# Second layer norm of a fused attention and MLP kernel: the turn of its rows moved from TensorE to VectorE, with the norm's scales passed through memory

## The chip, the cores and the metric

The kernel runs on one core of one Trainium2 chip. The metric is the device time of one execution in microseconds, median of several runs. Engines are named as the profile names them: PE is TensorE (PEld its weight loads), DVE is VectorE, ACT is ScalarE, POOL is GpSimd, SP is SyncE, which here only issues DMAs.

## The reference

One block of a transformer in f32, 2048 tokens of width 1024, 32 heads of 32, hidden width 3584:

```python
qkv = layernorm(x) @ wqkv
phi_q, phi_k = [softmax(t @ w_phi), softmax(-t @ w_phi)]  per head, t = q, k
o = (phi_q @ (phi_k^T v)) / (phi_q @ sum(phi_k) + 1e-6)
h = x + o @ wo
out = h + relu(layernorm(h) @ w1) @ w2
```

The layer norms have no weights: `(h - mean) / sqrt(var + 1e-5)` over the 1024 columns of a token. The change is in the second one, `layernorm(h)`.

## The kernel before, in words

**Matmuls.** Every product is made to f32 accuracy from two fp32r halves, a high part and a rest: `mm3` (L181) issues three matmuls of 512 columns, on L182, L183 and L184. Such a triple is called a step here. The work is a list of items, of 8 steps or (in the MLP) 4 steps each, in this order on PE: keys and values, queries, the output projection (`wo_item`, 32 items, the "wo stretch"), the up products of the MLP for token half b=0 and then b=1 (`up_item`, 98 items each), and the down products.

**What lies beside.** Everything else is hung on step numbers by a table: `when(step, f, ...)` (L904) calls f after that step of PE's list, and each engine gets its instructions in that order and runs them in order. `wo0` is the first step of the wo stretch, `up0` the first of the up products. What a step number fixes is therefore the order on each engine, and not a time: an instruction that waits holds up all behind it on its engine. SP issues nearly all DMAs in the same way, in one queue. The program gives each DMA one of eight semaphores in turn, so that a DMA waits for the landing of the one issued eight places before it.

**Attention inside the wo stretch.** For every pair of units u, POOL multiplies (`at_sums` L574, `at_den` L590, L594, `at_scale` L607, L612), DVE reduces (`at_reduce` L580), inverts (L597) and turns 32x32 blocks in place (`at_turn`, L618), then PE runs `at_num` (L632), ACT and DVE take its four banks (L639, L650). The chain goes POOL, DVE, POOL, DVE, POOL, DVE, PE. The last pair ends before the wo stretch does.

**Rows of h.** `wo_add` (L683, DVE) adds x to the projection in `xh`, `wo_store` writes it to memory (`hd`).

**Second layer norm before the change.** `ln_pair(b, i, stage)` (L691) does a pair of 128-token tiles, x1 and x2, four tiles of tokens apart; there are four pairs for each half b. Stage 0 reads both tiles back from `hd` (4 KB a token), stage 1 takes mean and variance (DVE, L221 and L223), stage 2 makes the two scales of a token (POOL, L230 to L232), stage 3 normalises (ACT, two instructions of 128x1024 on L238), stages 4 to 6 turn three half tiles and stage 7 the fourth: each is four 128x128 transposes on PE into one bank (L245, L713), copied back by ACT (L247, for b=0 L715 too). Stages 7 and 8 make sums and differences of quarters (DVE L717, L718, POOL L723, L724), since the MLP's products are made from seven combinations m of quarter matrices and not eight. `ln_store` writes the seven to memory (`hs`), `h_load` (L737) reads them into `hT[m]` in two parts g, `h_high` (ACT, L749) and `h_low` (DVE, L753) split them for the up products. The steps of the stages stand in the table `LN2` (L1050).

**Up products.** `up_item` keeps running sums in PSUM banks; ACT takes a bank (`up_take`, L776) after m = 1, 5, 6 and 4. After m=4 (the tile c21) the same bank is opened again one item later.

Of the kernel before, what the change touches and what calls it, by code (L numbers as in the profile page):

```python
# [140 lines left out]
def kernel(  # L141
# [60 lines left out]
    hs = {(b, m): dram.tile([P, 4, 512], F32, name=f"hs{b}_{m}") for b in range(2) for m in UP}  # L202
# [23 lines left out]
    def ln_power(key):  # L226

        mv = xst[key]
        sc = scx[:, key[1] - HT, :] if key[0] == "s" else lnp.tile([P, 2], F32, name="sc", bufs=4)
        pool.tensor_scalar_add(sc[:, 0:1], mv[:, 1:2], LN_EPS)  # L230
        pool.tensor_tensor(out=sc[:, 0:1], in0=sc[:, 0:1], in1=half, op=ALU.pow)
        pool.tensor_scalar(sc[:, 1:2], mv[:, 0:1], sc[:, 0:1], -1.0, op0=ALU.mult, op1=ALU.mult)  # L232
        xst[key] = sc

    def ln_norm(key):
        sc, src = xst.pop(("s", key[1]) if key[0] == "x" and key[1] >= HT else key), xin.pop(key)
        xnt[key] = src if key[0] == "h" else fp_ln.tile([P, D], F32, name="xn")
        act.activation(xnt[key], src, AF.Identity, bias=sc[:, 1:2], scale=sc[:, 0:1])  # L238

    def ln_turn(key, j, dst=None):  # L240
# [5 lines left out]
        if dst is None:  # L246
            act.activation(xn[:, j * 512:(j + 1) * 512], pt.rearrange("p k n -> p (k n)"), AF.Copy)  # L247
            return
# [441 lines left out]

    def ln_pair(b, i, stage):  # L691

        keys = [("h", HT * b + 4 * r + i) for r in range(2)]
        if stage == 0:
            for key in keys:
                ln_load(key, [hd[key[1]]])
        elif stage == 1:
            for key in keys:
                ln_stats(key)
        elif stage == 2:  # L700
            for key in keys:
                ln_power(key)
        elif stage == 3:
            for key in keys:
                ln_norm(key)
        elif stage in (4, 5, 6):
            ln_turn(keys[stage // 6], stage != 4)
        elif stage == 7:
            x1, x2 = (xnt[key] for key in keys)
            s12 = (mp or hp).tile([P, 2, 512], F32, name="s12", bufs=1)  # L710
            pt = tp_bank()
            for k in range(4):
                pe.transpose(pt[:, k * P:(k + 1) * P], x2[:, k * P:(k + 1) * P], ident)  # L713
            if b == 0:
                act.activation(s12[:, 1, :], pt, AF.Copy)  # L715
                pt = s12[:, 1, :]
            v.tensor_add(s12[:, 0, :], pt, x2[:, 512:])  # L717
            v.tensor_sub(x2[:, 0:512], x1[:, 0:512], pt)  # L718
            sums[b, i] = s12
        elif stage == 8:  # L720
            x1, s12 = xnt[keys[0]], sums[b, i]
            s4 = (mp or hp).tile([P, 512], F32, name="s4l", bufs=1)
            pool.tensor_tensor(out=s12[:, 1, :], in0=s12[:, 0, :], in1=x1[:, 0:512], op=ALU.subtract)  # L723
            pool.tensor_tensor(out=s4, in0=x1[:, 512:], in1=s12[:, 1, :], op=ALU.subtract)  # L724
            sums[b, i] = s12, s4

    def ln_store(b, i, j):

        x1, x2 = (xnt["h", HT * b + 4 * r + i] for r in range(2))
        s12, s4 = sums[b, i]  # L730
        m, t = ((1, x1[:, 0:512]), (5, s12[:, 0, :]), (6, s12[:, 1, :]), (2, x1[:, 512:]), (7, x2[:, 0:512]),
                (3, s4), (4, x2[:, 512:]))[j]
        sp.dma_start(hs[b, m][:, i, :], t)
# [3 lines left out]
    def h_load(b, m, g):  # L737

        lo = hT[m][:, 1, :, 2 * g * P:2 * (g + 1) * P].rearrange("p k (i n) -> p k i n", i=2)
        for i in range(2):  # L740
            sp.dma_start(f32(lo[:, :, i, :]), hs[b, m][:, 2 * g + i, :].rearrange("p (k n) -> p k n", k=4))
# [301 lines left out]
    for (t, hf), n in order:  # L1043
        do(max(n - 1, wo_first), -1, wo_load, t, hf)
        when(8 * n + (11 if n < wo_first + 2 else 9), wo_add, t, hf)
# [4 lines left out]
    LN2 = ((0, 9, 12, 17, 24, 25, 26, 27, 29, 36), (0, 18, 26, 32, 40, 42, 44, 46, 50, 60))  # L1050
    wo0 = 8 * wo_first
    up0 = 8 * first_up
    for i in range(4):
        for stage in range(9):
# [157 lines left out]
```

## Time and profile before

| what | value |
|---|---|
| median of 3 runs | 1896.47 us (1896.42 to 1900.21) |
| the profiled execution's own time | 1897.98 us |
| its span, first to last instruction | 1896.2 us |
| granted TensorE clock | 0.999 |
| busy: PE, DVE, POOL, ACT | 1880.8, 1050.0, 975.8, 740.3 us |
| wo stretch / b=0 up products begin | about 611 us / 818 us of the span |
| layer norm pairs, b=0 / b=1 | 664 to 803 us / 860 to 1054 us |

A row of the timeline gives start, duration, engine, line, operation, tiles and, in brackets, idle time before it and what ended that. A row of the grouped views ends in busy us, mean ns of one, and idle time before with its releasers. Consecutive matmuls overlap in the rows (0.39 us each, begun every 0.23 us), so that what a matmul takes of PE's time is the distance between starts.

### The profile page before, as it was taken

To read this page: it belongs to the slowest core of one execution; us is meant where nothing else is said; L and a number is where in the kernel's file an instruction comes from. 1 tells how busy PE (TensorE), PEld (TensorE's weight loads), DVE (VectorE), ACT (ScalarE), POOL (GpSimd) and SP (SyncE) were. 2 spreads that over 40 slices of the span, in tenths; PEclk is the share of its full clock that TensorE was granted. 3 is DMA by queue.
4 is the path that set the end of the run, shared out by engine and by line. 5 is a ranking of instruction groups with operands and counts; after the bars stand their busy time and mean duration, and the time that the engine had idled before them with its cause. 6 is when DMAs were issued, how large, how long until landed. Compare 5 with 4: busy or idle time off the path is not lost.

```text
span 1896.2 us, 31858 instructions
## 1 busy us (share of the span) xinstructions
PE 1880.8 (99%) x11640; PEld 1539.3 (81%) x11640; DVE 1050.0 (55%) x1685; ACT 740.3 (39%) x1258; POOL 975.8 (51%) x961
## 2 busy tenths in 40 slices
PE   8999999999999999999999999999999999999999
PEld 7777778877788788888888888888888888888887
DVE  6788678767679876555544563334433433343333
ACT  5322235222233112355445554444444444444442
POOL 4878742889946988423333222222244444444443
PEclk9999999999999999999999999999999999999999
DMA  6989785666665676796877996666677677777775
GB/s 222 285 280 310 232 284 197 194 192 209 199 207 177 199 240 221 248 272 219 272 233 238 301 285 202 181 194 202 217 240 217 198 234 236 239 212 219 216 216 178
DMA packets 292365, 432.17 MB, mean 228 GB/s; under 512 B 24048, under 2 KB 150000, under 8 KB 292208
## 3 DMA queue, kind: packets, MB, share of 16 engines
q1 hardware_dynamic: 275312, 413.36, 69.9%
q10 hardware_dynamic: 16896, 16.78, 2.5%
q8 instruction: 91, 1.49, 0.3%
q14 instruction: 66, 0.54, 0.1%
HBM read 292.68 MB, written 137.36 MB: 227 GB/s over the span
## 4 chain that ended last, share of the span: by engine, by line
PE 84%; POOL 6%; DMA 4%; issue 3%; DVE 2%; ACT 0%; SPq 0%; POOLq 0%; DVEq 0%; ACTq 0%
PE mm L182 21%; PE mm L183 21%; PE mm L184 21%; PE ac L184 4%; PE ac L182 4%; PE ac L183 4%; PE tp L182 2%; PE tp L184 2%; PE tp L183 2%; POOL w L129 2%; POOL b L361 2%; DMA b<-in_w_dram 1%; PE tp L245 1%; POOL ez L574 1%; DMA t<-b 1%
## 5 line engine op out<-in xcount | busy, mean ns | idle before, releaser
L129 POOL TENSOR_TENSOR w<-raw,w 128x512 fp32r<-128x512 f32 x355 | 475.2, 1340 | 722.0 <-ACT w L125 671.7
L125 ACT ACTIVATE w<-raw 128x512 fp32r<-128x512 f32 x686 | 409.1, 626 | 510.8 <-PE mm L184 245.4
L129 DVE TENSOR_TENSOR w<-raw,w 128x512 fp32r<-128x512 f32 x331 | 271.6, 821 | 529.4 <-ACT w L125 526.2
L182 PE MATMUL mm<-w,xT 128*128 128x512 f32 x768 | 308.5, 402 | 0.0
L183 PE MATMUL mm<-w,xT 128*128 128x512 f32 x768 | 301.5, 393 | 4.2 <-POOL w L129 3.8
L184 PE MATMUL mm<-w,xT 128*128 128x512 f32 x768 | 300.1, 391 | 0.0
L182 PE MATMUL mm<-hT,w 128*128 128x512 f32 x672 | 262.6, 391 | 0.0
L183 PE MATMUL mm<-hT,w 128*128 128x512 f32 x672 | 261.6, 389 | 0.3 <-DVE hT L753 0.3
L184 PE MATMUL mm<-hT,w 128*128 128x512 f32 x672 | 261.6, 389 | 0.0
L361 POOL TENSOR_TENSOR b<-b 128x256 f32<-128x256 f32 x224 | 181.1, 809 | 67.1 <-DMA b<-in_w_dram 57.6
L183 PEld LDWEIGHTS mm<-w,xT 128*128 128x128 f32 x768 | 144.7, 188 | 36.8 <-POOL w L129 7.3
L182 PEld LDWEIGHTS mm<-w,xT 128*128 128x128 f32 x768 | 144.6, 188 | 34.8 <-issue 4.2
L184 PEld LDWEIGHTS mm<-w,xT 128*128 128x128 f32 x768 | 144.6, 188 | 30.9
L182 PE MATMUL mm<-w 128*128 128x512 f32 x392 | 152.5, 389 | 0.0
L183 PE MATMUL mm<-w 128*128 128x512 f32 x392 | 152.5, 389 | 0.0
L184 PE MATMUL mm<-w 128*128 128x512 f32 x392 | 152.5, 389 | 0.0
L183 PEld LDWEIGHTS mm<-hT,w 128*128 128x128 f32 x672 | 126.2, 188 | 26.6 <-DVE hT L753 0.7
L184 PEld LDWEIGHTS mm<-hT,w 128*128 128x128 f32 x672 | 126.1, 188 | 26.3
L182 PEld LDWEIGHTS mm<-hT,w 128*128 128x128 f32 x672 | 126.2, 188 | 25.7
L452 POOL TENSOR_TENSOR zacc<-zacc,kphi 128x512 f32<-128x512 f32 x60 | 81.9, 1364 | 9.4 <-DVE kphi L444 9.4
L182 PEld LDWEIGHTS mm<-w 128*128 128x128 f32 x392 | 73.6, 188 | 15.3
L184 PEld LDWEIGHTS mm<-w 128*128 128x128 f32 x392 | 73.6, 188 | 15.3
(169 smaller groups left out, 3096.8 us busy)
## 6 DMA issues: line engine op xcount, KB each, us to landing
raw<-t SPq DMA_DIRECT2D x224, 256.0 KB, 4.0
raw<-ad SPq DMA_DIRECT2D x196, 256.0 KB, 3.0
raw<-in_w_dram SPq DMA_DIRECT2D x168, 256.0 KB, 3.1
b<-in_w_dram SPq DMA_DIRECT2D x56, 512.0 KB, 5.1
t<-b SPq DMA_DIRECT2D x56, 512.0 KB, 4.7
ad<-c SPq DMA_DIRECT2D x112, 256.0 KB, 3.6
ad<-s SPq DMA_DIRECT2D x84, 256.0 KB, 4.1
ed<-qe ACTq DMA_DIRECT2D x32, 512.0 KB, 4.6
```

Source lines behind the costliest of these rows:

```text
L125: nc.scalar.activation(w[:, 0, :], raw[1], AF.Copy)
L129: eng.tensor_tensor(out=w[:, 1, :], in0=raw[1], in1=w[:, 0, :].bitcast(F32), op=ALU.subtract)
L182: pe.matmul(ps, a_hi, b_hi, start=first, stop=False, skip_group_check=more)
L183: pe.matmul(ps, a_hi, b_lo, start=False, stop=False, skip_group_check=more)
L184: pe.matmul(ps, a_lo, b_hi, start=False, stop=last, skip_group_check=more)
L245: pe.transpose(pt[:, k, :], xn[:, (4 * j + k) * P:(4 * j + k + 1) * P], ident)
L361: pool.tensor_tensor(out=tsum[*u, *out], in0=tsum[*u, *a], in1=tsum[*u, *b], op=ALU.subtract)
L452: pool.tensor_tensor(out=zacc[s], in0=zacc[s], in1=phi_of[key], op=ALU.add)
L574: pool.tensor_tensor(out=ez, in0=e_q[u].rearrange("p (i h) s f -> p i (h s f)", i=4)[:, 2 * j:2 * j + 2, :], in1=zb[:, q, None, 256 * r:25 ...
```

## The change

The turn of the rows leaves PE. A tile is read back from `hd` in four DMAs of 32 partitions each, in pieces of 512 bytes, so that partition 32a+t gets the columns 128a to 128a+127 of each half of the row, for the four tokens 4t to 4t+3. DVE then turns the 32x32 blocks (`ln_swap`, one instruction of 128x1024 for each tile, written with a step of four elements), and the remaining exchange of chunks between partition groups is made by the addresses with which `h_load` reads `hs`: four DMAs of 32 partitions in place of two of 128. Since a partition now holds four tokens, mean and variance are taken earlier, on `xh` right after `wo_add` (`wo_stats`), the scales are made 4 steps later, written to memory four times over (`wo_scale`, 8 bytes a piece, into `scd`) and read back so that each partition has the scales of its four tokens (`scx`). ACT normalises in eight instructions of 128x256 for a pair. All sums stay, with other buffers as their places. The table `LN2` has new steps.

```diff
-    hs = {(b, m): dram.tile([P, 4, 512], F32, name=f"hs{b}_{m}") for b in range(2) for m in UP}
+    hs = {(b, m): dram.tile([P, 4, 4, P], F32, name=f"hs{b}_{m}") for b in range(2) for m in UP}
+    scd = {(b, i): dram.tile([2, 4 * P * 2], F32, name=f"scd{b}_{i}") for b in range(2) for i in range(4)}
...
+    def wo_stats(t, hf):
+        if hf == 0:
+            hst[t] = lnp.tile([P, 2, 6], F32, name="st", bufs=4)
+        v.bn_stats(out=hst[t][:, hf, :], in_=xh[t, hf])
+        if hf == 1:
+            xst["h", t] = mv = lnp.tile([P, 2], F32, name="mv", bufs=4)
+            v.bn_aggr(out=mv, in_=hst.pop(t))
+    def wo_scale(t):
+        dst = scd[t // HT, t % 4][t % HT // 4].rearrange("(a p s) -> p a s", a=4, s=2)
+        sp.dma_start(dst, xst.pop(("h", t))[:, None, :].to_broadcast([P, 4, 2]))
+    def ln_swap(dst, src):
+        v.transpose(dst.rearrange("p (c t g) -> p g c t", c=8, g=4), src.rearrange("p (g c k) -> p g c k", g=4, c=8))
     def ln_pair(b, i, stage):
...
+        if stage < 2:
+            t = tiles[stage]
+            xnt["h", t] = x = lnp.tile([P, D], F32, name="xin")
+            for a in range(4):
+                sp.dma_start(x[32 * a:32 * (a + 1)].rearrange("t (g r f) -> t g r f", g=4, r=2),
+                             hd[t].rearrange("(t g) (r a f) -> a t g r f", g=4, r=2, a=4)[a])
         elif stage == 2:
+            sp.dma_start(scx[:, 2 * i:2 * i + 2].rearrange("p r g s -> p r (g s)"),
+                         scd[b, i].rearrange("r (p f) -> p r f", f=8))
         elif stage == 3:
+            for r, t in enumerate(tiles):
+                for g in range(4):
+                    x, sc = xnt["h", t][:, 256 * g:256 * (g + 1)], scx[:, 2 * i + r, g]
+                    act.activation(x, x, AF.Identity, bias=sc[:, 1:2], scale=sc[:, 0:1])
+        elif stage == 4:
...
+            ln_swap(y2, x2)
+        elif stage == 5:
+            s, y1, y2 = sums[b, i]
+            ln_swap(y1, s)
+        elif stage == 6:
+            s, y1, y2 = sums[b, i]
+            v.tensor_add(s[:, 0:512], y2[:, 0:512], y2[:, 512:])
+            v.tensor_sub(y2[:, 0:512], y1[:, 0:512], y2[:, 0:512])
...
     def h_load(b, m, g):
-        for i in range(2):
-            sp.dma_start(f32(lo[:, :, i, :]), hs[b, m][:, 2 * g + i, :].rearrange("p (k n) -> p k n", k=4))
+        src = hs[b, m].rearrange("(a k) q i n -> q k a (i n)", a=4)
+        for q in range(4):
+            sp.dma_start(f32(hT[m][32 * q:32 * (q + 1), 1, :, 2 * g * P:2 * (g + 1) * P]),
+                         src[q, :, :, 2 * g * P:2 * (g + 1) * P])
...
+        when(added, wo_stats, t, hf)
+        if hf == 1:
+            when(added + 4, ln_power, ("h", t))
+            when(added + 12, wo_scale, t)
...
-    LN2 = ((0, 9, 12, 17, 24, 25, 26, 27, 29, 36), (0, 18, 26, 32, 40, 42, 44, 46, 50, 60))
+    LN2 = ((0, 3, 8, 16, 19, 21, 23, 25, 30), (0, 6, 10, 20, 26, 30, 34, 38, 46))
...
+        first, ln2 = wo0 + 64 + 40 * i, LN2[0] if i else (1, 4, 15, 21, 24, 26, 28, 30, 34)
```

On PE, where the turn of the first pair's tiles stood between the steps of a wo item, before (`tp<-ident,xin` are the transposes):

```order
L245 MATMUL tp<-ident,xin 128x128 x4
L182 MATMUL mm<-w,oT 128x512
L183 MATMUL mm<-w,oT 128x512
L184 MATMUL mm<-w,oT 128x512
L713 MATMUL tp<-ident,xin 128x128 x4
L182 MATMUL mm<-w,oT 128x512
```

In the changed kernel all 32 such rows are gone (7998 rows on PE in place of 8030), and nothing takes their place there.

On DVE, in the third pair of b=0, beside attention units 28 and 29 (`qe` their turn, `qtz` the reductions of the next two, `xh` the wo sums), before:

```order
L683 TENSOR_TENSOR xh<-mm,xh 128x512
L618 STREAM_TRANSPOSE qe<-qe 128x1024 x2
L683 TENSOR_TENSOR xh<-mm,xh 128x512
L580 TENSOR_REDUCE qtz<-ez 128x16 x2
L717 TENSOR_TENSOR s_8904<-s_8904,xin 128x512
L718 TENSOR_TENSOR xin<-xin,s_8904 128x512
L580 TENSOR_REDUCE qtz<-ez 128x16 x2
```

and in the changed kernel (`s_8880<-xin` and `xin<-xin` on L704 are the two swaps):

```order
L681 TENSOR_TENSOR xh<-mm,xh 128x512
L692 BN_STATS st<-xh 128x6
L704 STREAM_TRANSPOSE s_8880<-xin 128x4x256
L616 STREAM_TRANSPOSE qe<-qe 128x1024
L704 STREAM_TRANSPOSE xin<-xin 128x4x256
L616 STREAM_TRANSPOSE qe<-qe 128x1024
L733 TENSOR_TENSOR xin<-s_8880 128x512
L734 TENSOR_TENSOR s_8880<-xin,s_8880 128x512
L681 TENSOR_TENSOR xh<-mm,xh 128x512
L692 BN_STATS st<-xh 128x6
L695 BN_AGGR mv<-st 128x2
L578 TENSOR_REDUCE qtz<-ez 128x16 x4
```

Both swaps now stand ahead of an attention turn, and behind ACT's normalising.

On SP, just after the up products of b=0 have begun, where `hT7` and `hT3` are read for the first time (`raw` are weights), before:

```order
L741 DMA hT_9564<-hs_7_104 128x4x128 [waits DMAHW5_49,PE_49]
L741 DMA hT_9564<-hs_7_104 128x4x128 [waits DMAHW6_49]
L337 DMA raw<-t_2_312 128x512 [waits DMAHW7_49,Pool_49]
L741 DMA hT_9564<-hs_7_104 128x4x128 [waits DMAHW0_49]
L741 DMA hT_9564<-hs_7_104 128x4x128 [waits DMAHW1_49]
L337 DMA raw<-t_3_313 128x512 [waits DMAHW2_49,DVE_49]
L741 DMA hT_9565<-hs_3_105 128x4x128 [waits DMAHW3_49]
```

and in the changed kernel:

```order
L755 DMA hT_9630<-hs_7_104 32x4x256 [waits DMAHW0_49,PE_49]
L755 DMA hT_9630<-hs_7_104 32x4x256 [waits DMAHW1_49]
L755 DMA hT_9630<-hs_7_104 32x4x256 [waits DMAHW2_49]
L755 DMA hT_9630<-hs_7_104 32x4x256 [waits DMAHW3_49]
L335 DMA raw<-t_2_320 128x512 [waits DMAHW4_49,Pool_49]
L755 DMA hT_9630<-hs_7_104 32x4x256 [waits DMAHW5_49]
L755 DMA hT_9630<-hs_7_104 32x4x256 [waits DMAHW6_49]
L755 DMA hT_9630<-hs_7_104 32x4x256 [waits DMAHW7_49]
L755 DMA hT_9630<-hs_7_104 32x4x256 [waits DMAHW0_49]
L701 DMA scd_3_121<-sc 128x4x2 [waits DMAHW1_49]
L335 DMA raw<-t_3_321 128x512 [waits DMAHW2_49,DVE_49]
```

Each part g is four issues of 128 KB, in pieces of 1 KB, where it was two of 256 KB in pieces of 512 bytes; a scale write stands between them, and the turn of the eight DMA semaphores (DMAHW0 to 7) comes round after fewer bytes.

71 lines of the change are left out of this document (23 added, 48 removed).

## The prediction, as it was put on record before the run

> **What bounds the kernel now.** I read the page first: busy shares and slices.
>
> ```profile
> PE 1880.8 (99%) x11640; PEld 1539.3 (81%) x11640; DVE 1050.0 (55%) x1685; ACT 740.3 (39%) x1258; POOL 975.8 (51%) x961
> ...
> PE   8999999999999999999999999999999999999999
> ```
>
> PE is busy in 99% of the span and never under nine tenths after the first slice. Then who PE waits for, in the list of PE's waits:
>
> ```profile
> PE mm L183 <- POOL w L129: 3.8, 7, 1.4
> PE tp L245 <- ACT xn L238: 3.3, 2, 2.2
> ```
>
> These are the two largest entries of eight, 7.1 us. So PE's own instructions set the time, a microsecond off PE's list is a microsecond off the span, and the question is which waits grow. The same transposes grouped by form:
>
> ```profile
> L245 PE MATMUL tp<-ident,xin 128*128 128x128 f32 x96 | 14.4, 272 | 0.5 <-DVE oT L650 0.5
> L713 PE MATMUL tp<-ident,xin 128*128 128x128 f32 x32 | 4.8, 272 | 0.0
> ```
>
> Those 128 transposes, in 32 groups of four, are all that the change takes from PE.
>
> **What goes.** A row's duration is not its price, since matmuls overlap; the distance between starts is. PE's timeline at the first group:
>
> ```profile
> 681.32 0.39 PE L182 MATMUL mm<-w,oT 128*128 128x512 f32 x1
> 681.55 0.39 PE L183 MATMUL mm<-w,oT 128*128 128x512 f32 x1
> 681.78 0.40 PE L184 MATMUL mm<-w,oT 128*128 128x512 f32 x1
> 682.01 0.60 PE L245 MATMUL tp<-ident,xin 128*128 128x128 f32 x4
> 682.37 0.47 PE L182 MATMUL mm<-w,oT 128*128 128x512 f32 x1
> 682.68 0.39 PE L183 MATMUL mm<-w,oT 128*128 128x512 f32 x1
> ```
>
> From the L184 to the second matmul behind the group is 682.68 - 681.78 = 0.90 us; without a group two matmuls take 681.78 - 681.32 = 0.46 us. A group costs 0.44 us, four times 0.11 and not 0.27. 32 groups make 14.2 us, and the wait of 0.5 us for `oT` in the grouped row goes with them: **14.7 us** is the most that this edit can give.
>
> **What comes, engine by engine.** DVE gets two swaps a pair. The nearest row is the attention turn, the same operation on the same size, without the step of four elements in its output; beside it the sums that go on as they are and the statistics:
>
> ```profile
> L618 DVE STREAM_TRANSPOSE qe<-qe 128x1024 f32<-128x1024 f32 x28 | 34.3, 1232 | 15.8 <-POOL qe L612 14.6 <-POOL qe L602 1.2
> L221 DVE BATCH_NORM_STATS2 st<-xin 128x6 f32<-128x512 f32 x64 | 40.7, 676 | 7.9 <-DMA xin<-hd 7.0 <-DMA xin<-in_x_dram 0.8
> L223 DVE BATCH_NORM_AGGREGATE mv<-st 128x2 f32<-128x12 f32 x32 | 6.7, 209 | 1.4
> L718 DVE TENSOR_TENSOR xin<-xin,s 128x512 f32<-128x512 f32 x4 | 4.9, 1221 | 0.0
> ```
>
> No row shows the strided output. Below, a swap cannot take less than the 1.23 us of the dense one; above, the slower of the sums beside it has a mean of 1.22 us for 512 elements, 2.4 us for 1024. I take 1.23 us, the row of the same operation: 16 swaps, 19.7 us of DVE, up to 39. The Trainium skill, page "SBUF — State Buffer", section "Door 1: The DMA port swizzle (why `[64,N]` ≈ `[32,N]`)", says that SBUF is read in lines of 16 bytes and that every access to a new line pays; four f32 are one line, so by it each element of a swap pays. It gives no time, and no row here shows such a write. By it the sum below would end at the first rival's 1889.6 us, and without it at 1885.8.
>
> The statistics are as many as before, half of them (those of b=1) moved into the wo stretch: 16 on L692 and 8 small ones. ACT loses 24 copies of 0.6 us, with four more on L715, and has for the two normalising instructions of a pair (1.24 us each) eight of a quarter of the size:
>
> ```profile
> L247 ACT ACTIVATE xin<-tp 128x512 f32<-128x512 f32 x24 | 14.4, 599 | 19.5 <-PE tp L245 19.5
> L238 ACT ACTIVATE xin<-xin,sc 128x1024 f32<-128x1024 f32 x16 | 19.5, 1239 | 16.8 <-POOL sc L232 16.7
> L639 ACT ACTIVATE oT<-tp 128x256 fp32r<-128x256 f32 x32 | 10.6, 382 | 118.5 <-PE tp L632 113.0 <-PE ac L632 5.5
> ```
>
> A 128x256 one is between 0.31 us (a quarter) and 0.38 us; I take 0.38: 3.1 us a pair for 2.5. POOL's instructions are the same, the scales earlier. SP gets 128 more issues: 48 for the read-back, 16 scale writes, 8 scale reads, 56 for `hT`.
>
> **Three places where these can reach PE.**
>
> *Attention beside the pairs of b=0 (676 to 770 us).* Busy time by engine there:
>
> ```profile
> core 0: us, PE busy (x) PEld busy (x) DVE busy (x) ACT busy (x) POOL busy (x), PEclk, DMA share, GB/s
> 676.00:770.00 94.00, 93.51 (x1154) 75.80 (x1153) 65.06 (x113) 22.16 (x43) 81.66 (x105) 1.00 0.69 226
> 860.00:1050.00 190.00, 190.00 (x870) 157.37 (x869) 89.64 (x131) 94.34 (x155) 70.69 (x66) 1.00 0.74 237
> ```
>
> and, of the first of these stretches alone, the wo sums and the statistics:
>
> ```profile
> L683 DVE TENSOR_TENSOR xh<-mm,xh x14: 624/641/653, 680.0 to 768.9; 128x512 f32<-128x512 f32 x14
> L221 DVE BATCH_NORM_STATS2 st<-xin x8: 674/678/695, 705.8 to 742.9; 128x6 f32<-128x512 f32 x8
> ```
>
> Three pairs lie in the first stretch, so PE's list shrinks by 12 x 0.44 + 0.5 = 5.8 us to 88 us. POOL's 81.7 us stay: 93%. DVE gets six swaps (7.4 us) and, one for each wo sum, 14 statistics with 7 small ones for 8 with 4 (6 x 0.68 + 3 x 0.21 = 4.7 us): 65.1 + 12.1 = 77 us, 88%. Both still fit, but their chain has little slack; these are the turns of units 21 and 31 and the `at_num` that takes them:
>
> ```profile
> 698.11 1.25 DVE L618 STREAM_TRANSPOSE qe<-qe 128x1024 f32<-128x1024 f32 x1 [0.95 <-POOL qe L612]
> ...
> 767.76 1.25 DVE L618 STREAM_TRANSPOSE qe<-qe 128x1024 f32<-128x1024 f32 x1 [0.96 <-POOL qe L612]
> ```
>
> ```profile
> 700.93 0.34 PE L632 MATMUL tp<-qe,kvL 32*32 32x128 f32 x8
> ...
> 769.97 0.34 PE L632 MATMUL tp<-qe,kvL 32*32 32x128 f32 x8
> ```
>
> 700.93 - 699.36 = 1.6 us and 769.97 - 769.01 = 1.0 us. PE arrives 5.8 us earlier at the second. Part is made good: POOL stood idle here because DVE took statistics of rows still under way, and that place in DVE's list goes:
>
> ```profile
> 674.81 1.29 POOL L574 TENSOR_TENSOR ez<-qe,zb 128x512 f32<-128x512 f32 x1 [4.44 <-DVE qtz L580]
> ...
> 744.49 1.29 POOL L574 TENSOR_TENSOR ez<-qe,zb 128x512 f32<-128x512 f32 x1 [3.36 <-DVE qtz L580]
> ```
>
> Those two gaps are 7.8 us, more than the 4.8 us that lack (5.8 less the slack of 1.0); but a swap stands behind ACT, which stands behind two reads from memory, and all of DVE stands behind the swap, the next turn first. I leave **2 us** of the 5.8 lost here; the ends are 0 and all 5.8.
>
> *The first read of hT7.* It can only begin with the up products, and PE already waits for it by a hair:
>
> ```profile
> 839.72 0.39 PE L182 MATMUL mm<-hT,w 128*128 128x512 f32 x1
> 840.37 0.50 PE L183 MATMUL mm<-hT,w 128*128 128x512 f32 x1 [0.26 <-DVE hT L753]
> ```
>
> 840.37 - 839.72 is 0.65 us for 0.23. What is later by the change shows here at once; the bytes are the same, the issues double:
>
> ```profile
> hT<-hs SPq DMA_DIRECT2D x56, 256.0 KB, 6.1
> raw<-wpk SPq DMA_DIRECT2D x56, 128.0 KB, 3.3
> ```
>
> If a read of half the size lands like the other of 128 KB, in 3.3 us, eight places in flight carry as much as before. I put **1 us**, between 0 and 3.
>
> *ACT in b=1.* After m=4 ACT must empty the bank before PE opens it again:
>
> ```profile
> 1093.43 0.58 ACT L776 ACTIVATE c<-mm 128x512 f32<-128x512 f32 x1
> ```
>
> ```profile
> 1095.35 0.39 PE L182 MATMUL mm<-hT,w 128*128 128x512 f32 x1
> ```
>
> 1095.35 - 1094.01 = 1.3 us of slack. The third pair's eight normalising instructions are issued 4 steps (2.7 us) ahead of such a take and last 3.1 us, if rows and scales have landed; scales are asked for 10 steps (6.8 us) ahead. The second reads of hT, about 1063 to 1112 us, stand on ACT in the same way. **1 us** for both, between 0 and 4. In the rest of b=1 DVE has 190 - 90 = 100 us to spare, and the swaps cost nothing.
>
> **Sum.** 14.7 - 2 - 1 - 1 = 10.7 us. The profiled execution took 1897.98 us and would take 1887.3; it lies 1.5 us above the median, so that the median goes from 1896.47 to about **1885.8 us**. With the ends: 14.7 less 0 gives 1881.8, 14.7 less 12.8 gives 1894.6.
>
> **Rivals.**
>
> *The swaps go at half rate and DVE binds attention.* Where each element of a swap is a line of its own, 2.5 us a swap is twice the attention turn. DVE's 77 us become 85 of 88, and its waits for POOL (0.95 us before each second turn) find no room: the 5.8 us of that stretch come back whole. 14.7 - 5.8 - 1 - 1 = 6.9: **1889.6 us**. The rule on lines in the Trainium skill's page "SBUF — State Buffer" would have it so. For it speaks that nothing in the trace writes so; against it that DVE also gives up waits for rows from memory.
>
> *The eight places bind, and it is slower.* SP's rows for the first reads of hT7, hT3 and hT4 (16 DMAs, 12 of them `hT`) and for the second reads of all (59, 28 of them `hT`), first and last of each:
>
> ```profile
> 827.22 0.93 SPq L741 DMA_DIRECT2D hT<-hs  x2
> ...
> 838.47 1.04 SPq L741 DMA_DIRECT2D hT<-hs  x2
> ...
> 1063.79 2.47 SPq L741 DMA_DIRECT2D hT<-hs  x4
> ...
> 1111.91 1.10 SPq L741 DMA_DIRECT2D hT<-hs  x2
> ```
>
> They take 12 and 49 us now and will be 29 (12 more `hT`, a scale) and 87. If a landing took 6.1 us whatever the size, eight places would give 1.31 issues a us: 22 and 66 us, 10 and 17 us late. Weights are read far ahead; what `hT` has in hand I put at 3 us each time, so that PE loses 7 + 14 = 21 us. Against 14.7 less 2 that is 8 us slower, **1905 us**. It is no change at a landing of 5.5 us and slower from 5.8 on. The row of 3.3 us for 128 KB speaks against it; for it, that those went into 128 partitions and not 32.
>
> *The turn is not gone from PE's time.* Then the distance between matmuls there would stay and the time be 1896; the order has no row in the groups' place and PE has nothing else that waits, so I give it no more than 1 in 100.
>
> **Chances.** The forecast 0.63, with 1881.5 to 1889; DVE bound 0.18, up to 1893; still less than the forecast loses 0.04; the eight places, whole 0.07, in part 0.07; the turn not gone 0.01. About 0.2% (3.8 us) is what can be told from no change: faster 0.85, same 0.08, slower 0.07. The range leaves out the 0.15 above 1893 and a little below: 1881 to 1893.
>
> **What would show it.** PE's instructions fall to 11512, and where L245 and L713 stood starts are 0.23 us apart. The swaps' mean on L704 decides between 1.23 and 2.5 us. PE's waits at L632 name DVE or POOL if attention binds: 2 us in all by the forecast, 6 or more by the first rival. The landing of `hT<-hs` decides the second rival: 3.3 us or 5 and more, with PE's wait at the first matmul of m=7. At the openings of m=1 PE should wait under 1 us for ACT. I am wrong if PE waits 6 us at any one place, or if the swaps are past 2.4 us and L632 still waits for nothing.

## The result, and the profile after

The changed kernel takes **1946.28 us** (median of 4 runs, 1942.39 to 1949.42) against 1896.49 us (4 runs): a ratio of 1.0261, 95% interval 1.0249 to 1.0274. It is 50 us slower; 1885.8 had been forecast, with 1893 as the upper end. The profiled execution took 1949.42 us, its span is 1947.6 us and its mean granted clock 0.984 (0.999 before).

First the page of the changed kernel: PE's busy row, its slices and the granted clock in tenths.

```profile
PE 1891.1 (97%) x11512; PEld 1539.6 (79%) x11512; DVE 1085.4 (56%) x1701; ACT 736.2 (38%) x1278; POOL 974.2 (50%) x961
...
PE   8999999999999989979999999999999999999999
...
PEclk9999999999999989989999999999999999999999
```

The 128 transposes are gone (11512 instructions for 11640), yet PE's busy time has gone up by 10.3 us, since some of it went at a lower clock (below); and PE has two slices under nine tenths, at 682 and at 828 us, where before it had none after the first. Next, whom PE waits for (total, times, longest):

```profile
PE tp L630 <- issue: 10.5, 4, 6.9
PE mm L182 <- ACT c L791: 9.9, 4, 4.1
PE mm L182 <- ACT hT L764: 7.3, 2, 7.1
PE mm L182 <- DVE xh L681: 5.1, 2, 4.6
PE tp L630 <- DVE qe L616: 4.6, 4, 2.1
PE mm L183 <- POOL w L129: 3.4, 5, 1.4
PE mm L183 <- DMA hT<-hs: 2.7, 1, 2.7
```

Before, no entry was above 3.8 us. L630 is `at_num`, L764 and L768 the split of `hT`, L791 the taking of a bank. Where these waits lie, and what the DMAs move meanwhile, is shown by two stretches, the attention beside the pairs of b=0 and the first up products. Here they are in the changed kernel:

```profile
676.00:770.00 94.00, 81.96 (x959) 64.14 (x957) 63.15 (x102) 18.56 (x46) 69.06 (x83) 0.92 0.82 199
...
818.00:893.00 75.00, 59.17 (x232) 46.44 (x231) 34.16 (x40) 28.80 (x42) 21.38 (x22) 0.86 0.99 218
```

The second one before (the first stands in the prediction, with PE busy for 93.51 of 94 us):

```profile
818.00:893.00 75.00, 74.74 (x337) 61.57 (x336) 39.01 (x51) 41.26 (x65) 22.78 (x20) 1.00 0.81 246
```

PE loses 12 and 16 us there, at a clock of 0.92 and 0.86, and POOL and DVE do *less* in the first than before (69.1 for 81.7 us, 63.2 for 65.1). So DVE isn't overloaded: something makes all of them wait. The last two columns point to it: the DMA engines are busy for 82% and 99% of the time at 199 and 218 GB/s, where before 69% gave 226 and 81% gave 246. The same bytes take more of the engines' time.

**The attention wait, followed back.** PE's longest wait in the first stretch, from the timelines of PE, DVE, POOL, ACT and SP:

```profile
706.46 0.47 PE L630 MATMUL tp<-qe,kvL 32*32 32x128 f32 x8 [6.90 <-issue]
...
708.61 0.47 PE L630 MATMUL tp<-qe,kvL 32*32 32x128 f32 x8 [1.40 <-DVE qe L616]
```

```profile
692.13 2.00 DVE L704 STREAM_TRANSPOSE s<-xin 128x1024 f32<-128x1024 f32 x1 [10.64 <-ACT xin L722]
...
707.31 1.25 DVE L616 STREAM_TRANSPOSE qe<-qe 128x1024 f32<-128x1024 f32 x1 [0.95 <-POOL qe L610]
```

```profile
696.04 1.29 POOL L572 TENSOR_TENSOR ez<-qe,zb 128x512 f32<-128x512 f32 x1 [5.94 <-DVE qtz L578]
```

```profile
688.03 4.07 ACT L722 ACTIVATE xin<-xin,scx 128x256 f32<-128x256 f32 x8 [11.59 <-DMA xh<-in_x_dram]
```

```profile
663.70 7.24 SPq L713 DMA_DIRECT2D xin<-hd  x8
671.05 0.53 SPq L701 DMA_DIRECT2D scd<-sc  x1
...
672.95 0.37 SPq L701 DMA_DIRECT2D scd<-sc  x1
...
679.68 0.37 SPq L716 DMA_DIRECT2D scx<-scd  x1
```

Read from below: the scales are asked for at 679.68 us and ACT can only normalise at 688.03, some 8 us later. DVE has stood at the first swap since 681.5, the attention reductions (L578) behind it; POOL waits for those for 5.9 us, the turn of unit 21 ends at 708.56 and PE has waited since 699.6. The profile names "issue" and a read of `xh` as releasers. ACT doesn't use `xh`; of what it needs, the read of the scales came last, for it stands eight places behind the last read of the rows in SP's queue, so that those had landed when it was issued. A second read was late too: POOL had stood for 6.1 us, up to 686.34, for the attention's own read of `ed`. How much of PE's wait is due to which of the two this trace does not separate (a run below shows that late scales are enough).

**The first read of hT7.** The next large wait is at its first use:

```profile
876.40 0.80 PE L182 MATMUL mm<-hT,w 128*128 128x512 f32 x1 [7.11 <-ACT hT L764]
879.92 0.80 PE L183 MATMUL mm<-hT,w 128*128 128x512 f32 x1 [2.72 <-DMA hT<-hs]
```

```profile
863.35 5.31 SPq L755 DMA_DIRECT2D hT<-hs  x4
...
870.48 7.72 SPq L755 DMA_DIRECT2D hT<-hs  x8
```

Four and eight issues take 5.3 and 7.7 us, about a us each: SP waits at each for the landing of the one eight places before. The table of DMAs gives the landings (KB each, median us):

```profile
hT<-hs SPq DMA_DIRECT2D x112, 128.0 KB, 6.1
xin<-hd SPq DMA_DIRECT2D x64, 128.0 KB, 5.9
raw<-wpk SPq DMA_DIRECT2D x56, 128.0 KB, 3.7
scd<-sc SPq DMA_DIRECT2D x16, 4.0 KB, 8.4
scx<-scd SPq DMA_DIRECT2D x8, 8.0 KB, 6.5
```

A read of `hT` of half the size lands in the same 6.1 us as before, and a scale write of 4 KB, the smallest transfer of the program, takes the longest of these. Last, the two new groups on DVE and ACT:

```profile
L704 DVE STREAM_TRANSPOSE s<-xin 128x1024 f32<-128x1024 f32 x8 | 16.2, 2022 | 32.2 <-ACT xin L722 26.8 <-DMA hd<-xh 5.4
L722 ACT ACTIVATE xin<-xin,scx 128x256 f32<-128x256 f32 x64 | 32.5, 592 | 55.0 <-DMA scx<-scd 14.8 <-DMA xh<-in_x_dram 11.6 <-POOL ez L572 11.0
```

A swap takes 2.0 us, a normalising instruction 0.59.

**The clock.** After these waits PE goes slower for a while. The 13.7 us from 871.7 on, as a row of busy times, granted clock third from the end:

```profile
871.70:885.40 13.70, 6.28 (x14) 4.61 (x15) 5.76 (x7) 6.15 (x9) 1.80 (x1) 0.50 1.01 192
```

There matmuls begin 0.43 us apart instead of 0.23. Behind 600 us there are eight such stretches at 0.5, of 3.4 to 13.7 us, 61 us in all, each following one or more waits; before there was none. The account: the span grew by 51 us, and some 14 of saved transposes have to be added. PE's waits behind 600 us grew from 1.3 to 42.6 us, which makes 41 of these 65 us. For the other 24 there is the half clock: PE was busy for 44 of the 61 us, and half of that, an estimate of 22 us, is lost.

### The profile page after: what moved, and what is told of

Its sections match the earlier page's. It is cut to its first block, busy times and chain, and to the rows that moved or that the text cites. A ratio compares the mean times of both kernels' runs of the same rounds, so it can differ in the third digit from the quotient of the medians.

```text
span 1947.6 us, 31843 instructions
## 1 busy us (share of the span) xinstructions
PE 1891.1 (97%) x11512; PEld 1539.6 (79%) x11512; DVE 1085.4 (56%) x1701; ACT 736.2 (38%) x1278; POOL 974.2 (50%) x961
## 4 chain that ended last, share of the span: by engine, by line
PE 78%; DMA 9%; POOL 6%; issue 3%; DVE 2%; ACT 1%; SPq 1%; POOLq 0%; ACTq 0%; DVEq 0%
PE mm L182 19%; PE mm L183 19%; PE mm L184 19%; PE ac L184 3%; PE ac L183 3%; PE ac L182 3%; DMA hT<-hs 3%; PE tp L184 2%; PE tp L182 2%; PE tp L183 2%; DMA hd<-xh 2%; POOL b L359 1%; POOL w L129 1%; DMA xh<-in_x_dram 1%; POOL ez L572 1%
## 5 line engine op out<-in xcount | busy, mean ns | idle before, releaser
L129 DVE TENSOR_TENSOR w<-raw,w 128x512 fp32r<-128x512 f32 x331 | 276.4, 836 | 527.9 <-ACT w L125 527.5
L182 PE MATMUL mm<-hT,w 128*128 128x512 f32 x672 | 267.1, 398 | 22.4 <-ACT c L791 9.9
L183 PE MATMUL mm<-hT,w 128*128 128x512 f32 x672 | 265.8, 396 | 3.5 <-DMA hT<-hs 2.7
L184 PE MATMUL mm<-hT,w 128*128 128x512 f32 x672 | 265.1, 395 | 0.0
L182 PEld LDWEIGHTS mm<-hT,w 128*128 128x128 f32 x672 | 128.7, 192 | 53.0 <-ACT c L791 12.2
L183 PEld LDWEIGHTS mm<-hT,w 128*128 128x128 f32 x672 | 128.7, 192 | 31.6 <-DVE hT L768 4.3
L184 PEld LDWEIGHTS mm<-hT,w 128*128 128x128 f32 x672 | 128.6, 191 | 26.9
```

The lines of the kernel that those rows point to most:

```text
L129: eng.tensor_tensor(out=w[:, 1, :], in0=raw[1], in1=w[:, 0, :].bitcast(F32), op=ALU.subtract)
L182: pe.matmul(ps, a_hi, b_hi, start=first, stop=False, skip_group_check=more)
L183: pe.matmul(ps, a_hi, b_lo, start=False, stop=False, skip_group_check=more)
L184: pe.matmul(ps, a_lo, b_hi, start=False, stop=last, skip_group_check=more)
```

## The experiments

Theory 1: the scale writes, in pieces of 8 bytes, slow all other transfers. Theory 2: reads into 32 partitions land no faster for being smaller, and the eight semaphores bind (the second rival of the prediction). Theory 3: the swaps bind DVE (its first rival). Theory 4: each wait of PE costs a stretch at half clock besides.

### Each suspect taken out of the changed kernel

Without the scale writes (`scd` filled once from rows of x instead):

```diff
     def wo_scale(t):
-        dst = scd[t // HT, t % 4][t % HT // 4].rearrange("(a p s) -> p a s", a=4, s=2)
-        sp.dma_start(dst, xst.pop(("h", t))[:, None, :].to_broadcast([P, 4, 2]))
+        xst.pop(("h", t))
```

> The changed kernel without its 16 scale writes of 512 pieces of 8 bytes: the scales that ACT reads come from rows of x that are copied to scd once, early, so the true scales are left out; all reads, normalising and swaps stay. Theory 1 (the 8-byte writes slow every other transfer for several us each, reads come late and PE stalls): most of the loss goes, 1946 to about 1900 us, and the read of the scales no longer holds ACT for 7 us. Theory 2 (reads into 32 partitions land no faster for being smaller and the eight semaphores bind): 1935 or more. Theory 3 (the swaps at 2.0 us bind DVE): 1935 or more.

With the reads over 128 partitions (here `hT`; the rows likewise):

```diff
-            sp.dma_start(f32(hT[m][32 * q:32 * (q + 1), 1, :, 2 * g * P:2 * (g + 1) * P]),
-                         src[q, :, :, 2 * g * P:2 * (g + 1) * P])
+            sp.dma_start(f32(hT[m][:, 1, q, 2 * g * P:2 * (g + 1) * P]),
+                         hs[b, m][:, q, 2 * g:2 * (g + 1), :].rearrange("p i n -> p (i n)"))
```

> The changed kernel with the reads of hT and of the rows in as many DMAs and pieces of the same size, but each over 128 partitions and not 32, so the exchange of chunks is left out; the scale writes stay. Theory 1 (scale writes): 1935 or more, since those stay. Theory 2 (32 partitions): the landing of hT falls from 6.1 to 3 or 4 us and the time to about 1900 us. Theory 3 (swaps): 1935 or more.

And both edits:

> The changed kernel with both edits: no scale writes (true scales left out) and the reads over 128 partitions (exchange of chunks left out). Theories 1 and 2, each or together: 1886 to 1892 us, which is what the first sum gave. Theory 3 (the swaps at 2.0 us bind DVE): still above 1930, since they are unchanged.

| kernel | median us | to before (95%) |
|---|---|---|
| changed | 1946.28 | 1.0261 (1.0249 to 1.0274) |
| no scale writes | 1917.03 | 1.0103 (1.0088 to 1.0118) |
| reads over 128 partitions | 1931.23 | 1.0176 (1.0161 to 1.0192) |
| both | 1891.84 | 0.9979 (0.9964 to 0.9994) |

Neither theory alone: the writes are worth 29 us, the partitions 15, both 54; theory 1 had expected about 1900 us from the first run and theory 2 as much from the second. Together they take 10 more than their sum; why was not tried. Theory 3 falls, since with the same swaps the time is below that of before. With both gone the mean clock is 0.999 again.

### Each suspect put into the kernel before

The 16 scale writes alone, from a constant, read by nothing:

> The kernel before with nothing but the 16 scale writes added, 12 steps behind the sum of a tile, from a constant and read by nothing. Theory 1: each write slows the DMAs around it; with the rows of the layer norm as early as before the cost is 3 to 20 us, 1900 to 1916. Theories 2 and 3: 1896 to 1898, as before.

The reads of rows and `hT` in 32 partitions:

> The kernel before with the reads of hT in four DMAs of 32 partitions and pieces of 1 KB, and the rows of the layer norm read as the changed kernel does, in 32 partitions and pieces of 512 bytes; the turn stays on PE. The columns of a token are then in other partitions than its norm takes them for, so the rows are not the true ones. Theory 2 (reads into 32 partitions are late): 1903 to 1921 us. If they cost only together with the other parts: 1896 to 1899.

and of the two one at a time:

```diff
-        for i in range(2):
-            sp.dma_start(f32(lo[:, :, i, :]), hs[b, m][:, 2 * g + i, :].rearrange("p (k n) -> p k n", k=4))
+        for q in range(4):
+            r = slice(32 * q, 32 * (q + 1))
+            sp.dma_start(f32(hT[m][r, 1, :, 2 * g * P:2 * (g + 1) * P]), src[r, :, 2 * g * P:2 * (g + 1) * P])
```

> The kernel before with nothing changed but the reads of hT: four DMAs of 32 partitions and 1 KB pieces in place of two of 128 partitions and 512 B pieces. With the rows read so too it took 24 us more. If hT is what costs: 1910 to 1922 us; if the rows are: 1896 to 1900.

> The kernel before with nothing changed but the reads of the rows for the second layer norm: four DMAs of 32 partitions and 512 B pieces in place of one of 128 partitions and 4 KB; a token's columns are then in other partitions than its norm takes them for, so the rows are not the true ones. If the rows are what costs: 1908 to 1922 us; if hT is: 1896 to 1900.

| added to the kernel before | median us | before, same chip | ratio (95%) |
|---|---|---|---|
| 16 scale writes | 1922.34 | 1896.72 | 1.0130 (1.0112 to 1.0148) |
| rows and hT in quarters | 1921.35 | 1896.96 | 1.0131 (1.0115 to 1.0146) |
| hT in quarters | 1915.14 | 1897.09 | 1.0089 (1.0074 to 1.0105) |
| rows in quarters | 1902.34 | 1897.09 | 1.0029 (1.0018 to 1.0040) |

Sixteen writes of 4 KB that nobody reads cost 25.6 us, above the 3 to 20 that theory 1 had expected. What they do is seen in the stretch from 676 to 692 us, where the programs still stand at the same place; of the kernel before, of the changed one, and of before with the writes (DMA share and GB/s are last):

```profile
676.00:692.00 16.00, 16.00 (x199) 13.08 (x198) 11.87 (x20) 6.29 (x11) 14.99 (x23) 1.00 0.45 151
```

```profile
676.00:692.00 16.00, 16.00 (x191) 13.01 (x190) 5.00 (x9) 4.41 (x11) 7.81 (x7) 1.00 0.80 145
```

```profile
676.00:692.00 16.00, 15.39 (x130) 12.00 (x130) 9.80 (x18) 6.09 (x10) 11.00 (x18) 1.00 0.95 147
```

At the same 150 GB/s the engines are busy for 45%, 80% and 95%. The packet records say it directly. Against the usual time of a packet of its size in the kernel before (the median: 27 ns for 512 bytes, 84 for 2 KB, 159 for 4 KB), the packets of that stretch took, with the longest 8-byte piece of the whole run beside it,

```
                           all packets   longest 8-byte piece
before                     x 1.20        -
changed                    x 2.07        1049 ns
before + scale writes      x 2.46        1298 ns
changed, scales by SBUF    x 1.20          39 ns
```

(the last kernel comes below). Without the 8-byte pieces themselves the two middle rows are 2.0 and 2.2: the packets of the other transfers take twice as long. The reads in quarters cost mostly through `hT`, 18 us, the rows 5; the sum of the two is 23, and both together 24. They land so:

```profile
hT<-hs SPq DMA_DIRECT2D x112, 128.0 KB, 5.3
```

This is the kernel with `hT` in quarters alone: 5.3 us for 128 KB, where before 256 KB took 6.1. Twice the issues at nearly the same landing is what the second rival had priced. That it is the 32 partitions and not the number of issues is shown by the changed kernel without scale writes, with its reads into 32 partitions and then, in the kernel with both edits, with as many reads of the same size over 128:

```profile
hT<-hs SPq DMA_DIRECT2D x112, 128.0 KB, 5.7
```

```profile
hT<-hs SPq DMA_DIRECT2D x112, 128.0 KB, 4.1
```

The packet records show why they land late. A 1 KB piece of `hT` takes a median of 79 ns in the first of these two and 46 in the second. In the microseconds in which many of the pieces began (40 or more), the 16 engines had no time free in the first (their packets add up to 1.09 of the time, at 237 GB/s) and some in the second (0.92, at 297 GB/s). So the engines themselves were full. That the eight places bound as well, which is the rival's mechanism, is not shown: no run had more than eight.

### Is it the 8 bytes, the pieces, or memory?

Three kernels were to do the whole computation, with reads over 128 partitions and the scales passed in three ways:

> The whole computation is done. The reads of rows and of hT go over 128 partitions with the exchange kept (rows in two DMAs by column half, hT in four DMAs by source group), and the scales of a tile are written once, 128 pieces of 8 bytes in place of 512, each partition group reading the same copy. With all 512 pieces such reads gave 1931 us, without writes 1892. Theory A (each 8-byte piece costs the same): a quarter of 39 us stays, 1902 us. Theory B (a write of this kind costs something fixed, as the landing of it does): 1925 or more.

> The whole computation is done, reads over 128 partitions with the exchange kept; the scales go from SBUF to SBUF without memory in between: four DMAs a tile, each of 128 pieces of 8 bytes, 512 pieces a tile as in the changed kernel, and the reads of scd are gone. Theory C (it is writing 8 bytes to memory that slows the others): 1892 to 1897 us. Theory D (it is the number of small pieces, wherever they go): 1925 or more.

> The whole computation is done, reads over 128 partitions with the exchange kept; DVE turns the scales of a tile (32x32 blocks), and they go to memory in pieces of 128 bytes, 32 pieces a tile in two DMAs, from where each partition reads two pieces of 16 bytes. If small pieces written to memory were what cost the time: 1892 to 1897 us, as without the writes, and faster than the kernel before within its interval or equal to it. If any exchange of scales through memory costs it: 1920 or more.

They took 2092.72, 2060.95 and 2085.61 us (ratios 1.1028, 1.0863 and 1.0990, each within 0.0017): far worse than anything expected, and no answer on the scales. The new reads, which all three share, have a source of another shape, with a dimension of four outermost:

```diff
+        for a in range(4):
+            sp.dma_start(f32(hT[m][:, 1, a, 2 * g * P:2 * (g + 1) * P]),
+                         hs[b, m][32 * a:32 * (a + 1)].rearrange("k q i n -> q k (i n)")[:, :, 2 * g * P:2 * (g + 1) * P])
```

The up products of b=0 in the second of them, in the view by stretches:

```profile
818.00:893.00 75.00, 42.93 (x163) 33.14 (x162) 26.29 (x31) 18.20 (x27) 18.63 (x20) 0.80 0.57 169
```

PE stands still for 32 of 75 us and the DMA engines are busy for only 57%. In the packet records, while pieces of `hT` were under way in this kernel, there were exactly four for half of the time and never over eight; in the kernel with both edits there were up to 21. Such a read, with an outermost dimension of 4, seems to be spread over four of the 16 DMA engines; that it is the outermost dimension was not tried apart. The Trainium skill has it so: page "DMA: Bandwidth & Descriptors", section "Why a DMA increments its semaphore by 16 and not by 1", says that a DMA goes to the largest number of engines, up to 16, that divides the slowest dimension of both its sides, here four. The records agree, with four pieces under way. So the question was put again with the changed kernel's own reads. Scales straight from SBUF to SBUF:

```diff
+        sc = xst.pop(("h", t))
+        i, r = t % 4, t % HT // 4
+        for a in range(4):
+            sp.dma_start(scx[32 * a:32 * (a + 1), 2 * i + r], sc)
```

> The changed kernel with its own reads over 32 partitions, but the scales go from SBUF to SBUF without memory in between: four DMAs a tile of 128 pieces of 8 bytes, as many pieces as in the changed kernel; the eight reads of scd are gone. Theory C (writing 8 bytes to memory slows the others): 1912 to 1920 us, as without the writes. Theory D (small pieces, wherever they go): 1938 or more.

and through memory in wide pieces, after a turn on DVE:

```diff
+        for s in range(2):
+            sp.dma_start(scd[t // HT, t % 4][t % HT // 4, s].rearrange("a (q n) -> q a n", q=4),
+                         turned[s::32][:, None, :].to_broadcast([4, 4, 32]))
...
+        v.transpose(turned, stg)
```

> The changed kernel with its own reads over 32 partitions; DVE turns the scales of a tile, and they go to memory in 32 pieces of 128 bytes a tile in place of 512 of 8 bytes, and come back in pieces of 16 bytes. If it is the 8-byte pieces: 1915 to 1922 us, as without the writes. If it is the passage through memory as such: 1938 or more.

The first took 1914.63 us (1.0093, 1.0078 to 1.0108), as without the writes: theory C. As many 8-byte pieces, in four times as many DMAs, slow nothing when they go into SBUF (x 1.20 above, as before); it is writing them to memory that does. The same page of the Trainium skill, section "Specifications", says that transfers of under 512 bytes are read, modified and written, and its section "Why small descriptors are slow (HBM only)" that those between SBUF and SBUF are spared; these runs agree, for pieces of 8 bytes, that memory makes the difference, and do not show how. The second took 1931.83 us (1.0181, 1.0162 to 1.0201), between its two cases. Its packets are hardly slower (x 1.3 in the same stretch). Whether that is due to the size of its pieces or to their number, 32 a tile for 512, is open, since the kernel meant for this (the first of the three) gave no answer. But its scales come late; here is ACT's normalising in the first kernel and in the second:

```profile
L723 ACT ACTIVATE xin<-xin,scx 128x256 f32<-128x256 f32 x64 | 32.9, 592 | 14.2 <-DMA xin<-hd 8.4 <-POOL sc L232 3.4 <-DVE oT L648 2.3
```

```profile
L730 ACT ACTIVATE xin<-xin,sc 128x256 f32<-128x256 f32 x64 | 32.4, 588 | 48.7 <-DMA sc<-scd 31.9 <-DMA xh<-in_x_dram 9.6 <-DMA raw<-in_w_dram 7.3
```

In this second kernel PE is busy for 80.75 of the 94 us from 676 to 770, as little as in the changed kernel, and POOL waits there only 1.8 us for reads of `ed`, for 7.2 in the changed kernel: late scales are enough for the attention wait.

So the passage of the scales costs in two ways: the 8-byte writes slow the others, and a write with a read behind it is late for the steps of the table.

### The swaps

> The changed kernel without scale writes and with reads over 128 partitions (1892 us), and with the swap written densely, without the step of four elements: true scales, the exchange of chunks and the order within a row are left out. If the 0.75 us by which each swap is longer than the dense turn is what still lacks against the forecast of 1886: 1885 to 1888 us. If the remainder is elsewhere (ACT's normalising, the chain of reads): 1891 to 1893.

```profile
L706 DVE STREAM_TRANSPOSE s<-xin 128x1024 f32<-128x1024 f32 x8 | 9.9, 1241 | 10.2 <-ACT xin L724 8.7 <-DMA raw<-t 1.5
```

Dense, a swap takes 1.24 us as the attention turn does. The time was 1888.89 us (0.9955, 0.9938 to 0.9971) against 1891.84, between the two cases that were expected. The medians are 3 us apart, but the intervals overlap; the step of four elements costs some 3 us or nothing, and is not the loss.

### The wait and the clock

ACT was given more work ahead of a bank's reopening, to make PE wait where nothing else is disturbed:

```diff
                 when(up_step(b, p, m) + k, f, p % 2, *args)
+                if f is up_take and m == 4:
+                    for _ in range({(0, 6): 6, (1, 4): 4, (1, 10): 10}.get((b, p), 0)):
+                        when(up_step(b, p, m) + k, take_again, p % 2)
```

> The kernel before with ACT's taking of the c21 bank done over again, 6 more times in one place of b=0 and 4 and 10 more times in two places of b=1 (0.58 us each, with 1.3 us of slack before each): PE must wait there about 2.2, 1.0 and 4.5 us, 7.7 us in all. Theory 4 (a wait of PE over some 1.5 us is followed by several us at half clock): 5 to 10 us more than the waits, 1909 to 1914 us, and the granted clock falls behind the two longer waits and not behind the short one. Without it: 1904 us.

A miss: 1896.94 us (1.0003, 0.9994 to 1.0013), and PE does not wait for the added work. The bank that the c21 tile leaves isn't opened by m=1 one item later, as the description of the kernel and the prediction had it, but by the next m=5 three items later. So the slack was some 7 us and not 1.3. Then with more:

> The kernel before with ACT's taking of the c21 bank done over 16, 13 and 20 more times in three places (0.63 us each). As the run with 6, 4 and 10 showed, the bank is opened again three items later, about 7.4 us behind the first take, so PE should wait about 2.7, 0.8 and 5.2 us, 8.7 us in all. Theory 4 (a wait of PE over some 1.5 us is followed by 3.4 to 13.7 us at half clock, a shorter one is not): the granted clock falls behind the first and the third place only and the time is 1908 to 1917 us. Without it: 1905 us.

1912.25 us (1.0077, 1.0063 to 1.0090), within the range of theory 4, but not for its reason alone: in the profiled execution (1909.29 us, the shortest of the four) the waits alone make 10.1 us. PE's waits for the added work (total, times, longest), and the stretches around the first and the third of them:

```profile
PE mm L182 <- ACT c L779: 10.1, 3, 5.7
```

```profile
976.00:982.00 6.00, 2.83 (x12) 2.00 (x12) 1.48 (x3) 5.78 (x12) 0.00 (x0) 1.00 0.00 0
1329.40:1333.70 4.30, 0.25 (x2) 0.00 (x0) 0.00 (x0) 4.08 (x8) 0.00 (x0) 0.99 0.00 0
1333.70:1340.50 6.80, 5.16 (x12) 4.12 (x13) 5.12 (x7) 4.16 (x8) 1.59 (x1) 0.50 0.19 54
```

The first wait was of 3.2 us, which leaves 1.2 for the second. The clock stayed at 1.00 behind the first and was 0.50 for 6.8 us from within that of 5.7. There 12 matmuls began 0.43 us apart for 0.23, so that the half clock cost some 2.5 us. That a wait can cost more than itself is shown; the threshold of 1.5 us is not, and the length of a wait does not decide it alone: in the last kernel below a wait of 2.8 us left the clock at 1 and one of 1.6 us brought 3.4 us at 0.5. The moments at which the clock changes are not free either. In each trace they lie whole multiples of 3.41 us apart, and in steps of 3.41 us counted from them the wait of 3.2 us takes up 1.3 of one step and 1.8 of the next, while that of 5.7 us fills a whole one. The Trainium skill, page "TensorE: Matmul & The Clock Gate", section "What's actually happening", lets the clock fall after an idle window of about 3.4 us, windows that run on whatever the kernel does. That agrees with these two waits and with the steps; but in the changed kernel waits of 2.4 and 2.1 us, begun 3 us apart, brought 6.8 us at 0.50 although neither fills a step, which it doesn't explain. On what it depends beyond that stays open.

### Without both causes

The last kernel does the whole computation with the turn on DVE. `hd` gets its column chunks outermost, so that a tile comes back in one DMA over 128 partitions with 4 KB each; the rows of w1 stand in the order in which the features lie after the turn, so that the exchange falls away and `hT` is read as before; the scales go from SBUF to SBUF.

```diff
-    hd = [dram.tile([P, D], F32, name=f"hd{t}") for t in range(NT)]
+    hd = [dram.tile([4, P, 2, P], F32, name=f"hd{t}") for t in range(NT)]
...
+            sp.dma_start(x, hd[t].rearrange("a (t g) r f -> (a t) (g r f)", g=4))
...
-        "w1": np.asarray(inputs["B_w1"]).reshape(2, 4, P, NC, P).transpose(3, 0, 2, 1, 4)
+        "w1": np.asarray(inputs["B_w1"]).reshape(2, 4, 4, 32, NC, P).transpose(4, 0, 1, 3, 2, 5)
```

> The whole computation by the turn on VectorE, without both causes: h is stored with its column chunks outermost, so that a tile comes back in one DMA over 128 partitions; the rows of w1 stand in the order in which the features lie after the turn (its layout at launch, as for the other weights), so that the exchange of chunks falls away and hT is read as before the change; the scales go from SBUF to SBUF. If the two causes are all: 1887 to 1892 us, faster than the kernel before; with the swaps at 2.0 us that stay, 1889 by the dense run's 3 us. If another cost of the turn is hidden behind them: 1896 or more.

**1891.24 us** (median of 6 runs) against 1897.09: a ratio of 0.9968, 0.9957 to 0.9980, within the 1887 to 1892 expected. It beats both kernels, by 55 us and by 6. The first line of its page, three stretches, and its landings:

```profile
PE 1867.5 (99%) x11512; PEld 1526.6 (81%) x11512; DVE 1080.3 (57%) x1701; ACT 735.9 (39%) x1278; POOL 975.0 (52%) x961
```

```profile
676.00:770.00 94.00, 88.61 (x1223) 70.77 (x1221) 77.39 (x126) 17.50 (x45) 80.62 (x102) 1.00 0.71 229
...
818.00:893.00 75.00, 72.39 (x319) 59.25 (x318) 40.37 (x48) 40.13 (x68) 22.47 (x18) 1.00 0.77 226
893.00:1095.00 202.00, 202.00 (x893) 167.27 (x892) 113.81 (x136) 106.58 (x183) 60.82 (x44) 1.00 0.83 271
```

```profile
hT<-hs SPq DMA_DIRECT2D x56, 256.0 KB, 5.8
...
xin<-hd SPq DMA_DIRECT2D x16, 512.0 KB, 6.2
...
scx<-sc SPq DMA_DIRECT2D x64, 1.0 KB, 3.2
```

PE's busy time is 13.3 us below that of before, the clock is back, and what is lost now lies where the prediction looked for it.

## Why the prediction was wrong, point by point

The prediction's own sign of being wrong came: PE waited over 6 us at one place, 6.9 us at L630 and 7.1 us at the first use of `hT7`.

- **14.7 us for the turn: right but for a little.** PE's busy time fell by 13.3 us where nothing else changed the clock (1880.8 to 1867.5), and the instructions to 11512. (32 times 0.44 is 14.1, not 14.2.)
- **The scale writes: the step that failed first.** They were counted as 16 issues of SP among 128, with no price of their own, although no row of before showed a write of 8-byte pieces. The swap, which no row showed either, had been bounded from both sides; the writes were not. Alone they cost 25.6 us, in the changed kernel 29. None of the rivals had this.
- **"If a read of half the size lands like the other of 128 KB, in 3.3 us": failed, the second step.** It landed in 6.1 us, and in 5.1 to 5.7 in the kernels without scale writes. The row taken was of reads into 128 partitions; the doubt (32 and not 128) had been written down and given 0.07 whole and 0.07 in part. The second rival named the right transfers and nearly the right size: it put 21 us of lost time on `hT`, and `hT` in quarters alone cost 18. That is in part luck. It expected no change at a landing of 5.5 us, by the eight places alone, and the 18 us came at 5.3, where the DMA engines had no time free (their packets add up to 1.05 of the time while `hT` was read).
- **The first read of hT7: 1 us, 0 to 3.** It was 7.1 and 2.7 us of waits, with 13.7 us at half clock; without the two causes 2.4 us (75 - 72.39, less the 0.26 of before), within its ends.
- **Attention beside the pairs of b=0: 2 us, 0 to 5.8.** PE stood for 12 us. The chain was the one named (swap behind ACT behind two reads, all of DVE behind the swap), but its length was set by late reads, that of the scales above all. Without the causes 4.9 us are lost (94 - 88.61 less 0.49), within its ends, near the upper one.
- **The swaps at 1.23 us: mis-sized.** They take 2.0 us, 1.6 times the dense turn, between forecast and first rival. The rival's sign came, with some 17 us of waits at L630 where it had set 6 or more, but not its cause, that DVE then binds attention: in the kernels without the late reads PE stood in that stretch for as long with dense swaps (1.24 us) as with the others, 88.44 us busy of 94 for 88.33. The trace thus agrees with the rule of the Trainium skill, page "SBUF — State Buffer", section "Door 1: The DMA port swizzle (why `[64,N]` ≈ `[32,N]`)", only in that the strided write is slower.
- **ACT in b=1: 1 us, from a misread row.** The slack of 1.3 us was to the wrong opening; it is about 7 us. The normalising instructions take 0.59 us each, not 0.31 to 0.38, and still cost nothing there in the last kernel (202.00 of 202 us busy). In the changed kernel the condition "if rows and scales have landed" failed: PE waited 9.9 us for ACT's takes (L791), once when ACT had stood 6.8 us for scales, once when it had stood 8.2 us for a second read of `hT`.
- **The clock: left out.** Every wait was priced at its own length. About 24 of the 65 us lost came on top of the waits, most of them by the half clock.

With the measured terms the sum for the last kernel is 13.3 and the 0.5 us of the wait for `oT`, less 4.9 and 2.4: 6.5 us, and its span is 6.8 us shorter. These losses are read from the same run, so the agreement says that nothing else was lost, and not more. The prediction's account of PE was good; that of the DMAs was not.

## What to carry to other kernels

A transfer whose form the trace does not show is an unknown, however small it is: here 64 KB of scales, of 432 MB, cost more than the whole turn was worth. Compare DMA share with GB/s in the same stretch; where the share rises and the rate does not, look for the form of a transfer, its piece size and its partitions, before looking at the compute engines. Where both fall and PE waits, look at its outermost dimension. And ask whether an exchange of data has to be made at all: giving the weights the order that the turn leaves made it unnecessary.

## What the runs showed of the hardware that was not expected

- Writes of 8-byte pieces to memory, 512 to a DMA, made the other packets around them take 2.0 to 2.2 times their usual time, and single pieces up to 1.3 us; the same pieces from SBUF to SBUF took at most 39 ns and slowed nothing.
- A read of 128 KB into 32 partitions landed in a median of 5.1 to 6.1 us, over 128 partitions in 4.1; pieces of 1 KB of the former took a median of 76 to 79 ns, of the latter 46, and while they ran the DMA engines had no time free.
- Reads with an outermost dimension of 4 in their source had four packets under way for half of the time, and the kernels with them were 9 to 10% slower than before.
- PE's granted clock fell to 0.5 for 3.4 to 13.7 us at waits of some us, though not at every one: a lone wait of 3.2 us left it at 1. Its changes lie whole multiples of 3.41 us apart.
